# Strassen's blocks: the eight matmul units of the second FFN product stand in two groups of four in each step

## The chip, the cores and the metric

One core of one Trainium2 chip runs the kernel. The metric is the device time of one execution in microseconds, lower is better. In the profile, PE is the matmul engine (TensorE), PEld its weight loads, DVE the vector engine, ACT the scalar engine, POOL the engine that issues some DMAs, and SP the queue that issues the others.

## What is computed

The reference is a linear attention followed by a feed-forward network (FFN), in float32:

```python
# q, k, v: (8, 8, 576, 64)
q_s = exp(q - max(q, -1)); q_s /= sum(q_s, -1) + 1e-09      # per token
k_s = exp(k - max(k,  2)); k_s /= sum(k_s,  2) + 1e-09      # per column, over the sequence
kv = einsum('bhsd,bhse->bhde', k_s, v)
attn = einsum('bhsd,bhde->bhse', q_s, kv)
x = attn.transpose(0, 2, 1, 3).reshape(4608, 512)
h = x @ w_in                                  # (512, 2048)
g = h * (1.0 / (1.0 + exp(-1.702 * h)))
out = g @ w_out                               # (2048, 512)
```

## The kernel before

The 4608 tokens are worked on in nine blocks of 512 (`t` = 0 to 8). Each operand of the FFN is split into a high and a low part, and a product is three matmuls: high by high, high by low, low by high. While one block runs its FFN, the attention of the next block is computed between its matmuls.

A block's FFN has eight steps; a step handles two of the sixteen 128-wide slices of the hidden layer. In blocks 0 and 1 the first FFN product is plain (`plain1`). In blocks 2 to 8 (`t >= 2`, 56 steps) it is one level of Strassen's algorithm (`ffn1`): seven half-size products, numbered 6, 1, 2, 7, 5, 4, 3 in the order in which a step runs them, each of six matmuls of 256 columns (L889). They use only two PSUM banks, Y (bank 4) and Z (bank 5), in turn: 6 in Y, 1 in Z, 2 in Z, 7 in Y, 5 in Z, 4 in Y, 3 in Z, then the next step's 6 in Y and 1 in Z. Between two products in a bank a vector or scalar instruction reads the bank:

- after product 1, ACT copies Z to `tt` (L913), and DVE adds Y and that copy (L902, `tt<-bank,tt`);
- after product 2, ACT applies the activation to Z (L905, `g<-bank`); product 5 then starts Z anew;
- after product 7, DVE adds Y and the copy (L902, `tt<-bank,tt`); product 4 then goes on in Y;
- after products 5, 4 and 3, DVE adds the bank and a part of `tt` into `g` (L902, `g<-bank,tt`); the next products in these banks are 3, the next step's 6 and the next step's 1.

The activation (L905), the split into high part `gh` (L930, ACT) and low part `gl` (L933, DVE) follow. The second FFN product (`ffn2`) uses `gh` and `gl` one step later: eight units, one for each of four token groups `c` and two slices `jj`. A unit is three matmuls of 512 columns (L952) that add into bank `c` (0 to 3); these banks fill over the whole block and are copied out (L962) at its end.

The order of the program is made by a planner. Each piece of work is added with an engine, a cost, what it reads and writes, and a rank. The due time of a matmul piece is its place when all of them are sorted by rank. The planner then walks through time with the given costs: whenever an engine is free, the ready piece with the earliest due time goes next. Each engine executes its own list in that fixed order. The rank of a step is `R(t, step, off)`: 15 slots for each step, and `off` is a place among them. The seven products stand at slots 0, 1, 4, 6, 8, 10 and 12 (`OPS`), and the units of the step before at the values that `slots` gives:

```python
slots = iter((2, 2.3, 2.6, 6.3, 6.6, 10.3, 10.6, 13))
units = [(c, jj) for jj in range(2) for c in range(C)] if t < 2 else [(c, jj) for c in (2, 3, 0, 1) for jj in range(2)]
...
rank = R(t, step + 1, next(slots))
```

So in a step of `t >= 2` with nothing else between, the order before is 6, 1, three units, 2, 7, two units, 5, 4, two units, 3, one unit. The weights of the first product (`wj`, `wt`) lie in two sets of buffers that take turns from step to step (`wt0`, `wj00`, `wj01` and `wt1`, `wj10`, `wj11`).

Of the kernel before, what the change touches and what calls it, by code (L numbers as in the profile page):

```python
# [138 lines left out]
def efficient_attention_then_gelu_ffn(  # L139
# [168 lines left out]
    def R(t, step, off=0.0):  # L308
        return SLOTS * (NS * t + step) + off
# [7 lines left out]
    def slot(kind, p, jj):  # L317
        return f"wo{SLOT[kind][p]}{jj}"
# [38 lines left out]
    def next_tmp(n):  # L357
        nt[n] += 1
        i = nt[n] % n
        return (tmp[i] if i < 2 else wide[:, i - 2]), ("tmp", i)  # L360
# [36 lines left out]
    def pair(t, step):  # L397


        return NS - 1 - step if t % 2 else step  # L400
# [536 lines left out]
    def ffn2(t, step):  # L937
        p, gi = pair(t, step), step % 2
        ov = out[t * TB : (t + 1) * TB, :].rearrange("(p c) m -> p c m", c=C)
        slots = iter((2, 2.3, 2.6, 6.3, 6.6, 10.3, 10.6, 13))  # L940
        units = [(c, jj) for jj in range(2) for c in range(C)] if t < 2 else [(c, jj) for c in (2, 3, 0, 1) for jj in range(2)]
        opened = set()
        for c, jj in units:
            u, cs = c // 2, slice(c % 2 * P, (c % 2 + 1) * P)
            first_, last = step == 0 and c not in opened, step == NS - 1 and c in opened
            opened.add(c)

            def run(c=c, jj=jj, u=u, cs=cs, first_=first_, last=last):
                gx, gl = (gs[e][gi][:, jj, u, cs] for e in range(2))
                wh, wl = wo[p, jj][:, 0], wo[p, jj][:, 1]  # L950
                for e, (l, r) in enumerate(((gx, wh), (gx, wl), (gl, wh))):
                    nc.tensor.matmul(bank[c], l, r, start=first_ and e == 0, stop=last and e == 2)  # L952

            rank = R(t, step + 1, next(slots))
            reads = (("gs", gi, 0, u, jj), ("gs", gi, 1, u, jj), slot("wo", p, jj))
            plan.add("PE", 0.70, reads, (("bank", c),), rank, run)
            if not last:
                continue
            o, T = next_tmp(2)

            def run_o(c=c, o=o):
                (nc.vector.tensor_copy if c % 2 else nc.scalar.copy)(o, bank[c])  # L962

            def run_d(c=c, o=o):
                nc.sync.dma_start(out=ov[:, c, :], in_=o)

            plan.add("DVE" if c % 2 else "ACT", 0.65, (("bank", c),), (T,), rank - PRIOR, run_o)
            plan.add("SP", 0.4, (T,), (("out", t, c),), rank - PRIOR, run_d, size=P * DM * 4, lead=2.0)
# [49 lines left out]
    for t in range(NB):  # L1018
        if t > 1:
            at(R(t, -1, 0.5), lambda rank, t=t: x_split(t))  # L1020
        for step in range(NS):
            if t:
                at(R(t, step - 2, 0.2), lambda rank, t=t, step=step: load_kept(t, step))
            if t == 1:
                at(R(t, step, 0.1), lambda rank, step=step: sums(step))
            at(R(t, step), lambda rank, t=t, step=step: (plain1 if t < 2 else ffn1)(t, step))
            at(R(t, step + 1, 1), lambda rank, t=t, step=step: ffn2(t, step))
# [30 lines left out]
```

## Time and profile before

| | |
|---|---|
| median of 3 runs | 848.88 us (847.56 to 849.13) |
| the profiled execution | 847.62 us, of which the span on the core is 845.8 us |
| PE busy | 840.3 us, 99% of the span |
| DVE busy | 521.8 us, 62% |
| ACT busy | 482.7 us, 57% |
| granted PE clock | 0.999 of 2.4 GHz |

The profile is one execution. A matmul's row gives its start and a modelled end, so the pace of PE is read from start to start. A weight load belongs to the matmul behind it and runs while the matmul ahead of it streams.

### The profile page before, as it was taken

What the parts mean: (1) busy time and instruction counts of PE and PEld (TensorE: products, weight loads), DVE (VectorE), ACT (ScalarE), POOL (GpSimd) and SP (SyncE); (2) the same over time, 40 slices, a digit from 0 to 9 for tenths busy, and PEclk for the clock granted to TensorE, in tenths of its full rate; (3) what the DMA queues carried; (4) which work ended last, traced back from release to release, by engine and by line L of the source; (5) the groups of instructions that cost most, each with busy time, mean ns of one, the idle gap of its engine ahead of it and who ended that gap; (6) DMA issues with size and microseconds to landing.
All of it is one profiled execution on the core that took longest, in us unless ns stands there. A gap on an engine that the chain in (4) does not pass through costs nothing.

```text
span 845.8 us, 14761 instructions
## 1 busy us (share of the span) xinstructions
PE 840.3 (99%) x5685; PEld 723.8 (86%) x5685; DVE 521.8 (62%) x1077; ACT 482.7 (57%) x834; POOL 110.5 (13%) x179
## 2 busy tenths in 40 slices
PE   9999999999999999999999999999999999999997
PEld 5788778877898899889988998899988899899996
DVE  8998899989357753785368636664356533453333
ACT  6978968669239642874368634954366533353332
POOL 2001011210121001210131012101110011101110
PEclk9999999999999999999999999999999999999999
DMA  9998957891597339851895169524563165416541
GB/s 269 376 397 250 275 163 240 247 317 55 162 264 214 96 100 253 220 162 34 250 252 154 47 208 266 174 88 147 169 198 110 50 201 175 147 50 200 174 150 50
DMA packets 126278, 155.63 MB, mean 184 GB/s; under 512 B 75520, under 2 KB 104192, under 8 KB 119808
## 3 DMA queue, kind: packets, MB, share of 16 engines
q0 software_dynamic: 25248, 83.37, 32.3%
q1 hardware_dynamic: 100960, 71.32, 28.8%
q8 instruction: 45, 0.74, 0.4%
q14 instruction: 25, 0.20, 0.1%
HBM read 128.45 MB, written 26.21 MB: 183 GB/s over the span
## 4 chain that ended last, share of the span: by engine, by line
PE 99%; DMA 0%; DVE 0%; issue 0%; DVEq 0%
PE bank L952 47%; PE bank L889 33%; PE bank L842 11%; PE bank L669 3%; PE bank L748 2%; PE bank L727 2%; PE bank L304 2%; PE bank L621 1%; DMA out<-tmp 0%; DVE tmp L962 0%; DVE g L265 0%; DVE first L261 0%; DVEq L962 0%; DVE g L268 0%; DVE first L262 0%
## 5 line engine op out<-in xcount | busy, mean ns | idle before, releaser
L952 PE MATMUL bank<-w,gh 128*128 128x512 f32 x1152 | 360.1, 394 | 0.0
L952 PEld LDWEIGHTS bank<-w,gh 128*128 128x128 f32 x1152 | 199.6, 188 | 32.5 <-issue 1.9
L952 PE MATMUL bank<-w,gl 128*128 128x512 f32 x576 | 226.4, 393 | 0.0
L889 PE MATMUL bank<-xo,wt 128*128 128x256 f32 x1344 | 186.8, 281 | 0.0
L889 PEld LDWEIGHTS bank<-xo,wt 128*128 128x128 f32 x1344 | 177.1, 188 | 8.9
L905 ACT ACTIVATE g<-g 128x512 f32<-128x512 f32 x112 | 58.8, 525 | 167.1 <-DVE g L902 166.6
L889 PEld LDWEIGHTS bank<-xo,wj 128*128 128x128 f32 x1008 | 136.2, 188 | 11.1 <-ACT qt L718 1.3
L889 PE MATMUL bank<-xo,wj 128*128 128x256 f32 x1008 | 144.5, 279 | 0.0
L952 PEld LDWEIGHTS bank<-w,gl 128*128 128x128 f32 x576 | 108.3, 188 | 23.6
L902 DVE TENSOR_TENSOR g<-bank,tt 128x256 f32<-128x256 f32 x168 | 71.0, 423 | 89.5 <-PE bank L889 89.5
L410 POOL DMA_DIRECT2D wj<-kept x96 | 59.4, 619 | 468.7 <-PE bank L889 398.3
L933 DVE TENSOR_TENSOR gl<-g,gh 128x512 fp32r<-128x512 f32 x112 | 77.2, 689 | 69.7 <-ACT gh L930 69.7
L902 DVE TENSOR_TENSOR tt<-bank,tt 128x256 f32<-128x256 f32 x112 | 47.3, 422 | 115.7 <-PE bank L889 95.9
L842 PE MATMUL bank<-xp,wj 128*128 128x512 f32 x384 | 93.4, 393 | 0.0
L842 PEld LDWEIGHTS bank<-xp,wj 128*128 128x128 f32 x384 | 71.6, 188 | 18.2 <-issue 2.0
L930 ACT CAST gh<-g 128x512 fp32r<-128x512 f32 x112 | 69.6, 621 | 3.3
L905 ACT ACTIVATE g<-bank 128x256 f32<-128x256 f32 x56 | 21.6, 385 | 82.5 <-PE bank L889 82.2
L572 POOL PARTITION_ALL_REDUCE mx<-mx x32 | 27.6, 863 | 107.4 <-DVE mx L568 100.0
L410 POOL DMA_DIRECT2D wt<-kept_t x42 | 22.3, 530 | 128.1 <-PE bank L889 128.1
L913 ACT COPY tt<-bank 128x256 f32<-128x256 f32 x56 | 20.9, 373 | 24.4 <-PE bank L889 23.8
L905 ACT ACT_TABLE_LOAD x25 | 32.1, 1283 | 0.5
L718 ACT ACT_TABLE_LOAD x23 | 29.5, 1283 | 0.4
(101 smaller groups left out, 788.2 us busy)
## 6 DMA issues: line engine op xcount, KB each, us to landing
wt<-kept_t POOLq DMA_DIRECT2D x42, 1024.0 KB, 5.2
wj<-kept POOLq DMA_DIRECT2D x54, 512.0 KB, 3.6
wj<-kept POOLq DMA_DIRECT2D x42, 256.0 KB, 4.8
out<-tmp SPq DMA_DIRECT2D x36, 256.0 KB, 2.8
raw<-in_moe_w_in SPq DMA_DIRECT2D x16, 512.0 KB, 10.0
raw<-in_moe_w_out SPq DMA_DIRECT2D x16, 512.0 KB, 9.0
kept<-wj SPq DMA_DIRECT2D x16, 512.0 KB, 8.9
kept_t<-wt SPq DMA_DIRECT2D x8, 1024.0 KB, 4.9
```

The source lines that it names most:

```text
L410: "POOL", 1.0, (key,), (ring,), R(t, step - 2, off), lambda: nc.gpsimd.dma_start(out=out(), in_=src), size=size,
L572: nc.gpsimd.partition_all_reduce(flat, flat, P, bass_isa.ReduceOp.max)
L669: nc.tensor.matmul(pk[r0 : r0 + D, m, cols], lhs, rhs, start=c == 0, stop=c == len(one_) - 1, tile_position=(0, r0),)
L718: plan.add("ACT", act(e), (k,), (k,), rank, lambda y=y: nc.scalar.activation(y, y, AF.Exp), table="exp")
L842: nc.tensor.matmul(bank[bk], w[:, l, c, :], x[:, r], start=c == 0 and e == 0, stop=c == KC - 1 and e == 2)
L889: nc.tensor.matmul(ph[bk], w, x[:, r, c, :], start=opens and c == 0 and e == 0, stop=c == 1 and e == 2, skip_group_check=True,)
L902: return lambda: nc.vector.tensor_tensor(out=o, in0=ph[bk], in1=x, op=ALU.add)
L905: return lambda: nc.scalar.activation(o, x, AF.Gelu_apprx_sigmoid)
L913: vec("ACT", act(n), (ZB,), (A,), 2, lambda: nc.scalar.copy(a, ph[Z]))
L930: vec("ACT", act(2 * n), half, H, slot, lambda c=c, gh=gh: nc.scalar.copy(gh, c))
L933: nc.vector.tensor_tensor(out=gl, in0=c, in1=gh.bitcast(F32), op=ALU.subtract)
L952: nc.tensor.matmul(bank[c], l, r, start=first_ and e == 0, stop=last and e == 2)
```

## The change

One line of `ffn2`: for blocks with `t >= 2` the units get other slots, with four of them behind product 1 (slot 1) and four around slot 10 to 11, behind product 4 (slot 10). Blocks 0 and 1 keep the old slots.

```diff
     def ffn2(t, step):
         p, gi = pair(t, step), step % 2
         ov = out[t * TB : (t + 1) * TB, :].rearrange("(p c) m -> p c m", c=C)
-        slots = iter((2, 2.3, 2.6, 6.3, 6.6, 10.3, 10.6, 13))
+        slots = iter((2, 2.3, 2.6, 6.3, 6.6, 10.3, 10.6, 13) if t < 2 else (2, 2.3, 2.6, 2.9, 10.3, 10.6, 10.9, 11))
```

The planner turns this into a new order. The first place is PE in the last block, from product 2 to product 4 of a step. In the names, `bank5` is Z, `bank4` is Y, `xo10`, `xo4`, `xo5`, `xo6` are the inputs of products 2, 7, 5 and 4, and the rows of L952 are units (a unit is one row with `gh` and one with `gl`). Before:

```order
L889 MATMUL bank5_68<-xo10_1986,wj00_107 128x256 x6
L889 MATMUL bank4_67<-xo4_2053,wt0_1476 128x256 x6
L952 MATMUL bank3_66<-w_1109,gh1_78 128x512 x2
L952 MATMUL bank3_66<-w_1109,gl1_80 128x512
L952 MATMUL bank0_63<-w_1098,gh1_78 128x512 x2
L952 MATMUL bank0_63<-w_1098,gl1_80 128x512
L889 MATMUL bank5_68<-xo5_2058,wt0_1476 128x256 x6
L889 MATMUL bank4_67<-xo6_2064,wt0_1476 128x256 x6
```

The same place of the changed kernel, on PE:

```order
L952 MATMUL bank3_66<-w_1109,gh1_78 128x512 x2
L952 MATMUL bank3_66<-w_1109,gl1_80 128x512
L889 MATMUL bank5_68<-xo10_1986,wj00_107 128x256 x6
L889 MATMUL bank4_67<-xo4_2053,wt0_1476 128x256 x6
L889 MATMUL bank5_68<-xo5_2058,wt0_1476 128x256 x6
L889 MATMUL bank4_67<-xo6_2064,wt0_1476 128x256 x6
L952 MATMUL bank0_63<-w_1098,gh1_78 128x512 x2
L952 MATMUL bank0_63<-w_1098,gl1_80 128x512
```

The two units between products 7 and 5 are gone: one stands ahead of product 2 and one behind product 4, and the four products 2, 7, 5, 4 follow each other directly.

The second place is the border to the next step, on PE. `xo7` is the input of product 3; `xo8` and `xo9` are those of the next step's products 6 and 1. Before:

```order
L952 MATMUL bank1_64<-w_1098,gl1_80 128x512
L889 MATMUL bank5_68<-xo7_2079,wj01_108 128x256 x6
L952 MATMUL bank1_64<-w_1109,gh1_78 128x512 x2
L952 MATMUL bank1_64<-w_1109,gl1_80 128x512
L889 MATMUL bank4_67<-xo8_2011,wt1_1380 128x256 x6
L889 MATMUL bank5_68<-xo9_1792,wj10_109 128x256 x6
```

And of the changed kernel, on PE:

```order
L952 MATMUL bank1_64<-w_1109,gh1_78 128x512 x2
L952 MATMUL bank1_64<-w_1109,gl1_80 128x512
L889 MATMUL bank5_68<-xo7_2079,wj01_108 128x256 x6
L889 MATMUL bank4_67<-xo8_2011,wt1_1380 128x256 x6
L889 MATMUL bank5_68<-xo9_1792,wj10_109 128x256 x6
```

The unit between product 3 and the next product 6 now stands ahead of product 3, so that only product 6 lies between two products in bank Z.

The planner does not keep the pattern everywhere. The order of the changed kernel has products 2, 7, 5, 4 in direct sequence in 33 of the 56 steps. In 8 steps with attention work it has 2, 7, a unit, 4, a unit, 5; in 5 it has two units between 7 and 5; in the others a unit or attention matmuls stand between. Product 3, the next 6 and the next 1 follow directly at 25 step borders; at the others a unit, a transpose or attention matmuls stand between. SP's list is the same in both kernels, and POOL's differs in one exchange of neighbours in each of four blocks.

## Rows read from the trace of the kernel before

**Rows 1.** The page's head, the busy line, the granted PE clock in 40 slices (9 is 90% or more), and the chain of work that ended last, by engine.

```profile
span 845.8 us, 14761 instructions
PE 840.3 (99%) x5685; PEld 723.8 (86%) x5685; DVE 521.8 (62%) x1077; ACT 482.7 (57%) x834; POOL 110.5 (13%) x179
PEclk9999999999999999999999999999999999999999
PE 99%; DMA 0%; DVE 0%; issue 0%; DVEq 0%
```

**Rows 2.** The waits of PE and of its weight loads, longest first: us in total, times, longest us. "issue" is time without a wait that the profile shows.

```profile
PE bank L304 <- DVE g L268: 1.3, 1, 1.3
PEld bank L889 <- ACT qt L718: 1.3, 4, 0.5
PEld bank L889 <- issue: 0.8, 1, 0.8
```

**Rows 3.** Timeline of the last block, a step on the buffers `wt1`, `wj10`, `wj11` (start us, us, engine, line, operation, count; in brackets the idle time before and its releaser). In order: product 7, ACT's reading after product 2, the first unit, DVE's sum after product 7, products 5 and 4 in one row, the unit behind them, product 3, `gl`, the last unit, DVE's sum after product 3, the next product 6.

```profile
808.80 0.89 PE L889 MATMUL bank<-xo,wt 128*128 128x256 f32 x6
809.00 0.38 ACT L905 ACTIVATE g<-bank 128x256 f32<-128x256 f32 x1 [2.41 <-PE bank L889]
809.53 0.63 PE L952 MATMUL bank<-w,gh 128*128 128x512 f32 x2
809.73 0.42 DVE L902 TENSOR_TENSOR tt<-bank,tt 128x256 f32<-128x256 f32 x1 [2.67 <-PE bank L889]
...
810.91 1.60 PE L889 MATMUL bank<-xo,wt 128*128 128x256 f32 x12
...
812.36 0.63 PE L952 MATMUL bank<-w,gh 128*128 128x512 f32 x2
...
813.74 0.84 PE L889 MATMUL bank<-xo,wj 128*128 128x256 f32 x6
814.33 0.69 DVE L933 TENSOR_TENSOR gl<-g,gh 128x512 fp32r<-128x512 f32 x1 [1.35 <-ACT gh L930]
814.42 0.62 PE L952 MATMUL bank<-w,gh 128*128 128x512 f32 x2
...
814.94 0.42 DVE L902 TENSOR_TENSOR g<-bank,tt 128x256 f32<-128x256 f32 x1
815.11 0.84 PE L889 MATMUL bank<-xo,wt 128*128 128x256 f32 x6
```

**Rows 4.** The same view of the next step, on `wt0`, `wj00`, `wj01`: ACT's activation that follows DVE's sum of 814.94, product 1, ACT's reading after product 2, the first unit between 7 and 5, DVE's sum after product 7, products 5 and 4.

```profile
815.39 0.42 ACT L905 ACTIVATE g<-g 128x256 f32<-128x256 f32 x1 [1.09 <-DVE g L902]
815.79 0.84 PE L889 MATMUL bank<-xo,wj 128*128 128x256 f32 x6
...
819.41 0.39 ACT L905 ACTIVATE g<-bank 128x256 f32<-128x256 f32 x1 [2.37 <-PE bank L889]
819.89 0.62 PE L952 MATMUL bank<-w,gh 128*128 128x512 f32 x2
820.09 0.42 DVE L902 TENSOR_TENSOR tt<-bank,tt 128x256 f32<-128x256 f32 x1 [2.57 <-PE bank L889]
...
821.26 1.52 PE L889 MATMUL bank<-xo,wt 128*128 128x256 f32 x12
```

**Rows 5.** Timeline of the weight loads: those of the product 1 that starts at 815.79.

```profile
815.68 0.75 PEld L889 LDWEIGHTS bank<-xo,wj 128*128 128x128 f32 x6
```

**Rows 6.** Timeline of PE in a step on `wt0`, `wj00`, `wj01` that follows a stretch of attention matmuls: its product 6, its last unit (behind product 3), then the next step's products 6 and 1, where four transposes stand ahead of product 6.

```profile
417.98 0.87 PE L889 MATMUL bank<-xo,wt 128*128 128x256 f32 x6
...
427.77 0.63 PE L952 MATMUL bank<-w,gh 128*128 128x512 f32 x2
...
428.83 0.95 PE L889 MATMUL bank<-xo,wt 128*128 128x256 f32 x6
429.62 0.87 PE L889 MATMUL bank<-xo,wj 128*128 128x256 f32 x6
```

**Rows 7.** Five steps as stretches, each from the start of its product 6 to that of the next: the stretch, its length, busy time and rows of PE, PEld, DVE, ACT, POOL, then granted clock, DMA share and GB/s. The fourth uses `wt1`, `wj10`, `wj11`, the others `wt0`, `wj00`, `wj01`; the first and the last row are the first and the last of the fast steps that the prediction counts.

```profile
283.54:293.80 10.26, 10.26 (x68) 9.27 (x67) 6.38 (x15) 6.28 (x10) 0.48 (x1) 1.00 0.35 121
...
742.58:752.83 10.25, 10.25 (x68) 9.27 (x66) 6.84 (x14) 6.65 (x13) 0.00 (x0) 1.00 0.01 2
752.83:763.08 10.25, 10.25 (x67) 9.27 (x66) 4.68 (x10) 4.26 (x9) 1.31 (x3) 1.00 0.39 125
763.08:773.59 10.51, 10.51 (x68) 9.48 (x66) 4.00 (x9) 3.05 (x6) 1.79 (x4) 1.00 0.73 219
...
815.11:825.36 10.25, 10.25 (x67) 9.27 (x66) 3.31 (x8) 3.05 (x6) 0.48 (x1) 1.00 0.33 113
```

**Rows 8.** Timeline of a step with attention work, in the third block: DVE's sum after product 7, the second of two units behind product 7, then product 4 (which stands ahead of product 5 here).

```profile
266.04 0.42 DVE L902 TENSOR_TENSOR tt<-bank,tt 128x256 f32<-128x256 f32 x1 [1.17 <-PE bank L889]
...
266.52 0.62 PE L952 MATMUL bank<-w,gh 128*128 128x512 f32 x2
...
267.21 1.58 PE L889 MATMUL bank<-xo,wt 128*128 128x256 f32 x12
```

**Rows 9.** Timeline of the end of the program: the last `gl`, and the first of the last four units, which need it.

```profile
837.25 0.69 DVE L933 TENSOR_TENSOR gl<-g,gh 128x512 fp32r<-128x512 f32 x1 [1.14 <-ACT gh L930]
...
838.62 0.62 PE L952 MATMUL bank<-w,gh 128*128 128x512 f32 x2
```

## Prediction, made before the changed kernel ran

> **What bounds the kernel now.** I read the page first. PE is busy for 840.3 of 845.8 us, the clock is granted in full in every slice, and the chain that ended last is PE for 99% [rows 1]. The list of waits says the same from the other side: the only waits of PE and of the loads for the products with a named releaser come to 1.3 us each over the whole run [rows 2]. So in the 56 Strassen steps PE goes from matmul to matmul, and no other engine holds it. Two things follow. An order that does the same matmuls has no wait to remove, so it can gain little. And it can lose wherever it brings a product so close to the reader of its bank that PE has to wait. The rest is a question of how much room each product has, which the timelines of two quiet steps tell [rows 3, 4].
>
> A step takes 10.25 us on one set of weight buffers and 10.51 us on the other [rows 7]. I call them the fast and the slow pace; on the slow one a product lasts 0.72 us (810.91 to 812.36 for two), on the fast one 0.68 (815.11 to 815.79) [rows 3, 4].
>
> **What the change moves.** No instruction is added or removed. In front of product 5 two units go away, in front of the next product 6 one unit. What each product has left is the time from the end of the bank's reader to the start of the product, less the units taken out.
>
> *Product 5 waits for ACT's reading after product 2.* Slow step: ACT ends at 809.38, product 5 starts at 810.91, so there are 1.53 us; the two units take 1.38 (809.53 to 810.91); 0.15 is left [rows 3]. Fast step: 819.80 to 821.26 is 1.46, the units 1.37; 0.09 is left [rows 4].
>
> *Product 4 waits for DVE's sum after product 7.* Slow step: DVE ends at 810.15, product 4 starts one product after 810.91, at 811.63: 1.48 less 1.38 leaves 0.10 [rows 3]. Fast step: 820.51 to 821.94 is 1.43, less 1.37 leaves 0.06 [rows 4].
>
> *The next product 1 waits for DVE's sum after product 3.* DVE ends at 815.36, product 1 starts at 815.79: 0.43. Here DVE came late because `gl` held it till 815.02, while product 3 ended at 814.58; with a start 0.04 behind that end it would be 0.32 earlier. In the new order product 3 stands two units (1.38 us) further behind product 4, from which `gl` descends, so `gl` is out of the way. The unit taken out is 0.69 (814.42 to 815.11). 0.43 + 0.32 - 0.69 = 0.06 is left [rows 3, 4]. Where the product 6 between runs at the slow pace, 0.04 more: 0.10.
>
> **What a product needs.** No row shows PE waiting for ACT or DVE in such a place, so the cost is bounded from its parts. From the end of one engine's work to the start of another's that waited for it: 0.03 (815.36 to 815.39) [rows 3, 4]; with what rounding hides I take 0.04. The list of waits puts what PE waited for in the products on the weight load, not on the matmul [rows 2]. So the first load of a product is held too, and a load starts 0.11 us ahead of its matmul (815.68 to 815.79) [rows 4, 5]. That makes 0.15 us from the reader's end to the product's start. The lower bound is 0.04, if the load can go ahead of the wait. The upper bound is 0.25: behind four transposes product 6 takes 0.79 us (428.83 to 429.62) where 0.70 to 0.72 is usual, some 0.1 more for a break in the flow [rows 6].
>
> **The stalls.** With 0.15, a slow step loses 0 at product 5 and 0.05 at product 4. A fast step loses 0.06 at product 5, and at product 4 0.09 less the 0.06 already lost, 0.03. That is 0.07 a step on average; 33 steps have the four products in direct sequence: 2.3 us. Product 1 loses 0.09 or 0.05, on average 0.07; 25 borders: 1.8 us. In the 8 steps with 7, a unit, 4, the sum after product 7 ended at 266.46 and product 4 started at 267.21, 0.75 later; less one unit of 0.69 (266.52 to 267.21) leaves 0.06, so 0.09 is lost [rows 8]: 0.7 us. Three half cases (attention matmuls next to product 5) add 0.2. Sum 5.0 us.
>
> **The pace.** The second term is what a stall does behind itself. The fast buffers do not always run fast: the step at 417.98, on the fast set, follows attention matmuls that broke the flow, and from its product 6 to its last unit it takes 9.79 us (417.98 to 427.77) [rows 6]. At the fast pace that stretch is a step of 10.25 less its last unit of 0.69, 9.56 [rows 3, 7]. So a break leaves the step 0.23 us slower than the fast pace. By the starts and lengths of the products in the timeline fifteen steps, from the one at 283.54 to that at 815.11, run fast from product 6 on [rows 7]. If a stall acts like that break, they lose 0.23 each, less some 0.06 since on the slow pace the stalls are smaller: 15 x 0.17 = 2.6 us. I take it as likelier than not, as both hold the weight loads up; the bounds are 0 and 2.6.
>
> **What costs nothing.** The units wait for `gh` and `gl`; those of groups 0 and 1 move later, and those of groups 2 and 3 behind the same product 1, so none gets closer. At the end of the program product 3 moves 0.69 later, and with it the chain to the last `gl`, which loses the 0.3 us for which DVE was held; so `gl`, which ended at 837.94, would end at 838.3. The unit that needs it still starts at 838.62 and reads it in its third matmul [rows 9]. The weight DMAs that POOL issues wait for products 4 and 3; these move by one unit, 0.69, within a step of 10 us [rows 7]. Where the planner puts ACT's table loads ahead of the reading of product 2, it has kept four pieces between 2 and 5 as before.
>
> **Sum.** 5.0 + 2.6 = 7.6 us, of which 0.3 comes back since on the slow pace the first unit behind products takes 0.01 longer and there are two such borders instead of three (about 30 steps): 7.3. The profiled execution took 847.62 us, 1.8 above its span and 1.26 below the median of 848.88. On the profiled time that is 854.9, on the median 856.2; I say **856.0**.
>
> **Rivals.** *No wait at all.* If the weight load goes ahead and only the matmul waits, 0.04 is enough, less than the smallest room of 0.06. Nothing changes: 848.5 to 849.5. The rows speak against it, as they book the waits on the load [rows 2]; for it, that a load does run under the matmul ahead. The Trainium skill (TensorE: Matmul & The Clock Gate, Architectural detail) says that PE's queue can pull a weight load ahead of matmuls in flight, which favours this rival; no row here shows a load more than one matmul ahead. Chance 0.10.
>
> *A break costs more.* With 0.25 instead of 0.15, a slow step loses 0.15 at products 5 and 4 together, a fast one 0.19, product 1 0.19 or 0.15, the 8 steps 0.19: 33 x 0.17 + 25 x 0.17 + 8 x 0.19 = 11.4 us, with the pace 14: 863. For it speaks that PE has not once been seen to restart from such a wait, against it that the 0.1 was seen with a change of matmul shape. The Trainium skill (Perfetto Trace Analysis, Optimizing Tensor Performance) says that independent matmul groups should rotate through PSUM banks so that one's evacuation overlaps the next's matmuls; with two banks and one product between, that overlap is what gets short here. By that rule the change loses, but it gives no size. Chance 0.20.
>
> *Faster.* If a stall puts the slow steps on the fast pace instead, up to 28 steps gain 0.26 each, 7.3 us, against 5.0 of stalls: 846.5. It decides from 20 steps on (5.0 / 0.26). Against it speaks the broken step, which went to the slow side [rows 6]. Chance 0.04.
>
> **Numbers.** My forecast (5 to 9 us lost) has 0.66, and 856.0 is its time; its own range is 853 to 859. The range over the cases is 850 to 864, which leaves out the first and the third rival. A change of 0.2% (1.7 us) is about what a measurement of this kernel can tell from none. Slower by more: 0.66 + 0.20 = 0.86; the same: 0.10; faster: 0.04.
>
> **What would show it.** PE's list of waits would show L889 waiting for ACT g L905 and DVE tt and g L902, some 33 to 60 times each, under 0.15 us each. In a quiet step of the last block product 5 would start 0.15 us behind ACT's end and product 4 0.16 behind DVE's. The steps on the fast buffers would go from 10.25 to about 10.5 to 10.6, the slow ones from 10.51 to 10.6. If the waits are there but the steps on the fast buffers lose only the stalls, the pace term is wrong; if no waits are there, the load did go ahead. A long wait in the attention steps would mean that ACT or DVE came late there, which I cost at nothing.

## The result, and the profile after

The changed kernel takes 854.52 us (median of 6 runs, 853.75 to 854.71) where the kernel before takes 848.90 on the same chip (6 runs, 847.56 to 849.13): a ratio of 1.0070, 95% interval 1.006 to 1.008. It is slower, by 5.6 us. The profiled execution took 853.75 us.

The page of the changed kernel, its head, the busy line and the chain of work that ended last:

```profile
span 852.0 us, 14765 instructions
PE 846.4 (99%) x5685; PEld 729.1 (86%) x5685; DVE 522.9 (61%) x1077; ACT 479.1 (56%) x834; POOL 117.7 (14%) x179
PE 99%; DMA 0%; DVE 0%; issue 0%; DVEq 0%
```

Against [rows 1] the span is 6.2 us longer, and PE is "busy" for 6.1 us more with the same 5685 matmuls. So the page shows no idle engine: the loss is booked as busy time. The steps show it. Three of the last block as stretches (columns as in [rows 7]): a step on `wt0`, `wj00`, `wj01`, one on the second set, and the next on the first set.

```profile
778.55:789.12 10.57, 10.57 (x69) 9.55 (x67) 3.42 (x7) 3.01 (x6) 1.79 (x3) 1.00 0.54 174
810.29:820.88 10.59, 10.59 (x68) 9.57 (x67) 3.42 (x7) 3.02 (x6) 1.79 (x3) 1.00 0.56 169
820.88:831.44 10.56, 10.56 (x68) 9.53 (x67) 3.42 (x7) 3.01 (x6) 0.71 (x1) 1.00 0.25 83
```

Before, the first set's steps took 10.25 and the second set's 10.51 [rows 7]; they lost 0.31 and 0.08, and the two sets now run alike, at a granted clock of 1.00 as before.

Where it went, product by product. The timeline of the slow step 810.29: ACT's reading after product 2, then the first weight load of product 5; DVE's sum after product 7, then the first load of product 4 (start us, us, engine, line, operation, count; in brackets the idle time before and its releaser):

```profile
815.43 0.38 ACT L905 ACTIVATE g<-bank 128x256 f32<-128x256 f32 x1 [3.07 <-PE bank L889]
815.87 0.19 PEld L889 LDWEIGHTS bank<-xo,wt 128*128 128x128 f32 x1
816.15 0.42 DVE L902 TENSOR_TENSOR tt<-bank,tt 128x256 f32<-128x256 f32 x1 [3.07 <-PE bank L889]
816.62 0.19 PEld L889 LDWEIGHTS bank<-xo,wt 128*128 128x128 f32 x1
```

At the next border: product 6, DVE's sum after product 3, then the first loads of product 1 and its six matmuls.

```profile
820.88 0.84 PE L889 MATMUL bank<-xo,wt 128*128 128x256 f32 x6
821.08 0.42 DVE L902 TENSOR_TENSOR g<-bank,tt 128x256 f32<-128x256 f32 x1 [0.97 <-PE bank L889]
821.56 0.30 PEld L889 LDWEIGHTS bank<-xo,wj 128*128 128x128 f32 x2
821.56 0.98 PE L889 MATMUL bank<-xo,wj 128*128 128x256 f32 x6
```

And in the fast step that follows, again product 5 behind ACT and product 4 behind DVE:

```profile
826.01 0.39 ACT L905 ACTIVATE g<-bank 128x256 f32<-128x256 f32 x1 [3.07 <-PE bank L889]
826.45 0.19 PEld L889 LDWEIGHTS bank<-xo,wt 128*128 128x128 f32 x1
826.70 0.42 DVE L902 TENSOR_TENSOR tt<-bank,tt 128x256 f32<-128x256 f32 x1 [3.02 <-PE bank L889]
827.18 0.19 PEld L889 LDWEIGHTS bank<-xo,wt 128*128 128x128 f32 x1
```

Add start and length of each reader: it ends at 815.81, 816.57, 821.50, 826.40 and 827.12, and the load starts 0.06, 0.05, 0.06, 0.05 and 0.06 later. Five times out of five, on ACT and on DVE, the load is what waits. Before, the load of product 1 began at 815.68, 0.32 behind DVE's end at 815.36 [rows 3, 5], and in the same quiet steps products 5 and 4 started 1.4 us and more behind their readers [rows 3, 4]. Product 1's row shows the loss of a border in one number: its six matmuls last 0.98 where they lasted 0.84 [rows 4].

The list of waits of the weight loads hardly shows it (us in total, times, longest):

```profile
PEld bank L889 <- DVE tt L902: 2.0, 8, 0.3
```

These eight are the steps "7, a unit, 4, a unit, 5", for instance this load of product 4:

```profile
267.84 0.77 PEld L889 LDWEIGHTS bank<-xo,wt 128*128 128x128 f32 x6 [0.25 <-DVE tt L902]
```

The list counts idle time from the end of the load before, so it books 0.25 where only some 0.08 is lost (product 4 lasts 0.78 to 0.81 there, not 0.71 or 0.72); and the waits of 0.02 to 0.11 us at products 1, 5 and 4 of the other steps it doesn't list at all. A load's row lasts 0.19 and the next load starts 0.11 to 0.12 behind its start, so when a load is late by that little, the one ahead of it still counts as running or has ended at most 0.03 before.

### The profile page after: what moved, and what is told of

It reads as the page before. It is cut to its first block, busy times and chain, and to the rows that moved or that the text cites. A ratio compares the mean times of both kernels' runs of the same rounds, so it can differ in the third digit from the quotient of the medians.

```text
span 852.0 us, 14765 instructions
## 1 busy us (share of the span) xinstructions
PE 846.4 (99%) x5685; PEld 729.1 (86%) x5685; DVE 522.9 (61%) x1077; ACT 479.1 (56%) x834; POOL 117.7 (14%) x179
## 4 chain that ended last, share of the span: by engine, by line
PE 99%; DMA 0%; DVE 0%; issue 0%; DVEq 0%
PE bank L952 47%; PE bank L889 33%; PE bank L842 10%; PE bank L669 3%; PE bank L748 2%; PE bank L727 2%; PE bank L304 2%; PE bank L621 1%; DMA out<-tmp 0%; DVE tmp L962 0%; DVE g L265 0%; DVE first L261 0%; DVEq L962 0%; DVE g L268 0%; DVE first L262 0%
## 5 line engine op out<-in xcount | busy, mean ns | idle before, releaser
L952 PE MATMUL bank<-w,gh 128*128 128x512 f32 x1152 | 359.8, 393 | 0.0
L952 PEld LDWEIGHTS bank<-w,gh 128*128 128x128 f32 x1152 | 204.8, 188 | 39.2 <-issue 4.1
L952 PE MATMUL bank<-w,gl 128*128 128x512 f32 x576 | 226.2, 393 | 0.0
L889 PE MATMUL bank<-xo,wt 128*128 128x256 f32 x1344 | 186.5, 284 | 0.0
L889 PEld LDWEIGHTS bank<-xo,wt 128*128 128x128 f32 x1344 | 172.0, 188 | 4.2 <-DVE tt L902 2.0
L889 PEld LDWEIGHTS bank<-xo,wj 128*128 128x128 f32 x1008 | 137.5, 188 | 11.5 <-issue 0.8
L889 PE MATMUL bank<-xo,wj 128*128 128x256 f32 x1008 | 146.4, 280 | 0.0
L952 PEld LDWEIGHTS bank<-w,gl 128*128 128x128 f32 x576 | 108.2, 188 | 23.8
L902 DVE TENSOR_TENSOR g<-bank,tt 128x256 f32<-128x256 f32 x168 | 70.8, 423 | 78.3 <-PE bank L889 76.5
L902 DVE TENSOR_TENSOR tt<-bank,tt 128x256 f32<-128x256 f32 x112 | 47.1, 421 | 110.9 <-PE bank L889 94.8
L572 POOL PARTITION_ALL_REDUCE mx<-mx x32 | 35.4, 1105 | 106.5 <-DVE mx L568 99.4
L731 ACT COPY qT<-bank 128x512 f32<-128x512 f32 x36 | 20.7, 582 | 18.2 <-PE bank L727 17.8
```

What stands on the lines that cost most here:

```text
L572: nc.gpsimd.partition_all_reduce(flat, flat, P, bass_isa.ReduceOp.max)
L731: plan.add("ACT", act(TB), (PB,), (Q,), rank, lambda: nc.scalar.copy(qT[hp % 2], pq), lead=-2.5)
L889: nc.tensor.matmul(ph[bk], w, x[:, r, c, :], start=opens and c == 0 and e == 0, stop=c == 1 and e == 2, skip_group_check=True,)
L902: return lambda: nc.vector.tensor_tensor(out=o, in0=ph[bk], in1=x, op=ALU.add)
```

## The experiments

Seven steps of the last block, from the first set's step in which product 6 stands at 752.83 before to the one at 825.36, have no attention matmuls, so they are the yardstick: 72.53 us before, by these two starts [rows 7]. The same stretch in the changed kernel (columns as in [rows 7]):

```profile
757.50:831.44 73.94, 73.94 (x464) 66.81 (x463) 26.08 (x52) 22.66 (x45) 10.73 (x18) 1.00 0.52 164
```

In the first experiment:

```profile
756.82:830.18 73.36, 73.36 (x463) 66.37 (x462) 26.62 (x52) 22.47 (x46) 10.73 (x18) 1.00 0.53 165
```

In the second:

```profile
756.05:829.14 73.09, 73.09 (x464) 65.92 (x463) 25.90 (x52) 22.66 (x45) 10.73 (x18) 1.00 0.54 166
```

In the third:

```profile
755.00:827.54 72.54, 72.54 (x464) 65.52 (x462) 26.62 (x52) 22.50 (x46) 10.73 (x18) 1.00 0.53 167
```

**Only the places behind products 7 and 5.** Diff against the changed kernel:

```diff
-... else (2, 2.3, 2.6, 2.9, 10.3, 10.6, 10.9, 11))
+... else (2, 2.3, 2.6, 2.9, 10.3, 10.6, 10.9, 13))
```

> The last unit goes back to its old place between product 3 and the next step's product 6; the four units behind product 1, and with them product 5 and product 4 right behind products 7 and 5, stay as in the change. Theory of the bank waits: product 1 has a unit between its bank's reader and itself again, so its loss (2.6 us over the 56 steps between before and after) goes and that of products 5 and 4 (3.7 us) stays: 851.5 to 852.5 us, and a fast step of the last block goes from 10.56 to about 10.45. Rival, that the units in groups of four cost and not the waits: the groups are hardly changed, 854 to 855.

Measured: 852.66 us against 848.09 of the kernel before (ratio 1.0052, 1.0037 to 1.0067), a little above what I expected. The seven steps cost 0.83 more than before. A step on the first set and one on the second, as stretches:

```profile
756.82:767.22 10.40, 10.40 (x68) 9.40 (x67) 4.89 (x9) 4.19 (x10) 1.31 (x3) 1.00 0.46 137
767.22:777.75 10.53, 10.53 (x67) 9.53 (x66) 4.20 (x8) 3.05 (x7) 1.78 (x4) 1.00 0.75 233
```

The first set's step lost 0.15, not 0.31. The timeline of its matmuls, product 2, then products 7, 5 and 4 in one row, the unit behind them, product 3 and the unit behind it:

```profile
760.92 0.84 PE L889 MATMUL bank<-xo,wj 128*128 128x256 f32 x6
761.60 2.34 PE L889 MATMUL bank<-xo,wt 128*128 128x256 f32 x18
763.78 0.63 PE L952 MATMUL bank<-w,gh 128*128 128x512 f32 x2
...
765.85 0.84 PE L889 MATMUL bank<-xo,wj 128*128 128x256 f32 x6
766.53 0.62 PE L952 MATMUL bank<-w,gh 128*128 128x512 f32 x2
```

Product 2 takes 0.68 from start to start, and so does product 3. The three between take 2.18, 0.14 more than three times 0.68: the two stalls are 0.09 of that, and the rest is that products 5 and 4 run at the slow pace behind them. The rival of the groups put this run at 854 to 855, and the time is against it. But the group behind product 4 has one unit fewer here, so the run with another bank below, in which no unit moves, is the cleaner test.

**Only the border.**

```diff
-... else (2, 2.3, 2.6, 2.9, 10.3, 10.6, 10.9, 11))
+... else (2, 2.3, 2.6, 6.3, 6.6, 10.3, 10.6, 11))
```

> The reverse of the first: two units go back between product 7 and product 5, and the last unit stays ahead of product 3, so that only product 6 stands between product 3 and the next product 1. Theory of the bank waits: only product 1 loses, 25 to 33 times about 0.1 us: 851 to 852 us, and the two halves (this one less before, the first one less before) add up to the 5.6 us of the whole change. Rival, that one stall of a step already puts the rest of it on the slow pace: this one alone costs 4 us or more (853 and above) and the halves add up to more than the whole.

Measured: 851.57 us (1.0035, 1.0023 to 1.0048). Seven steps: 0.56 more. The two halves, 0.83 and 0.56, make 1.39 of the whole change's 1.41, so in quiet steps they add up and nothing is left for a third cause. The rival of one stall that slows the whole step falls there. The totals do not add up: 4.6 and 3.5 us make 8.1, not 5.6, which is what the rival had said. In the profiled executions the 56 steps come to 4.8 and 2.3 us more than before, against 5.6 for the whole change; another 1.5 us of this run arose ahead of them, where the program is the same (the first Strassen step starts at 215.32, in the first experiment at 213.82). So 1.5 us of the steps' sum lie outside the seven quiet ones, among them the steps whose attention work the planner orders differently in each version; where they arise was not traced.

**One unit at each place.**

```diff
-... else (2, 2.3, 2.6, 2.9, 10.3, 10.6, 10.9, 11))
+... else (2, 2.3, 2.6, 6.3, 10.3, 10.6, 10.9, 13))
```

> Three units behind product 1, one between 7 and 5, three behind 4, one behind 3: one unit of 0.69 us at each of the places that the change empties, where two stood between 7 and 5 before. Theory of the bank waits: one unit is more than the 0.16 us that a restart wants, no product waits, 848.5 to 849.5 us. Rival, that each unit taken from between 7 and 5 costs its share: half of the 3.7 us of products 5 and 4, 850.5 to 851.

Measured: 849.74 us, a ratio of 1.0017 (1.0008 to 1.0026), between the two expectations. The seven steps settle it: 72.54, not 0.02 more than before, with one unit fewer between 7 and 5. The rival falls. The rest lies outside them. In one step with attention work, which took 0.70 more than before, the planner put product 2 straight behind product 1 in the same bank. There the wait is long enough to be shown; the timeline of that run, with ACT's copy after product 1 and the load of product 2:

```profile
274.11 0.37 ACT L913 COPY tt<-bank 128x256 f32<-128x256 f32 x1 [1.34 <-PE bank L889]
...
274.53 0.77 PEld L889 LDWEIGHTS bank<-xo,wj 128*128 128x128 f32 x6 [0.67 <-ACT tt L913]
```

The load starts 0.05 behind ACT's end at 274.48, the same turnaround. What the other steps with attention work add was not traced.

**Another bank for products 5 and 3.** In the last block banks 6 and 7 are idle, so the reader of Z can be taken out of the way without moving any instruction:

```diff
+        Z5 = 6 if t == NB - 1 else Z
...
+            bk = Z5 if n in (5, 3) else bk
...
-        vec("DVE", dve(n), (ZB, TU), ((*GB, 1),), 9, plus(cb[:, 1], Z, u))
+        vec("DVE", dve(n), (ZB5, TU), ((*GB, 1),), 9, plus(cb[:, 1], Z5, u))
...
-        vec("DVE", dve(n), (ZB, TS), ((*GA, 1),), 13, plus(ca[:, 1], Z, s))
+        vec("DVE", dve(n), (ZB5, TS), ((*GA, 1),), 13, plus(ca[:, 1], Z5, s))
```

> The changed kernel, but in the last block, where bank 6 is idle, products 5 and 3 write to bank 6 in place of their own bank. So products 5 and 1 of the eight steps of that block have no reader to wait for; product 4 still waits for the sum after product 7. Order unchanged. Theory of the bank waits: product 1 goes from 0.82 to 0.71 us in a fast step (0.79 to 0.68 in a slow one), product 5 loses its 0.065, product 4 takes that on itself (0.02 to 0.09): a step of the last block takes 10.45 to 10.50 in place of 10.56 to 10.61. Rival, that the loss comes from the order itself (a flow broken by the place of the products): the steps of the last block stay at 10.56 to 10.61.

Measured (the time, 853.05 us, is of a single execution). Three steps of the last block as stretches, on the first, the second and the first set:

```profile
799.53:809.93 10.40, 10.40 (x69) 9.37 (x67) 3.42 (x7) 2.95 (x6) 1.79 (x3) 1.00 0.59 180
809.93:820.40 10.47, 10.47 (x68) 9.48 (x67) 3.42 (x7) 2.95 (x6) 1.79 (x3) 1.00 0.57 175
820.40:830.80 10.40, 10.40 (x68) 9.37 (x67) 3.42 (x7) 2.95 (x6) 0.71 (x1) 1.00 0.26 85
```

With the order of the changed kernel and only the bank changed, the steps give back 0.16 and 0.12, about half of what the order had cost on the first set and more on the second, which now takes 10.47 where it took 10.51 before the change. The timeline of the same run (its L904 and L891 are L902 and L889 of the others): the sum after product 7 and the first load of product 4, then, at the border, the sum after product 3 and the first loads of product 1:

```profile
826.07 0.42 DVE L904 TENSOR_TENSOR tt<-bank,tt 128x256 f32<-128x256 f32 x1 [2.88 <-PE bank L891]
826.55 0.19 PEld L891 LDWEIGHTS bank<-xo,wt 128*128 128x128 f32 x1
...
831.00 0.42 DVE L904 TENSOR_TENSOR g<-bank,tt 128x256 f32<-128x256 f32 x1 [0.97 <-PE bank L891]
831.40 0.31 PEld L891 LDWEIGHTS bank<-xo,wj 128*128 128x128 f32 x2
```

Product 1's load now starts at 831.40, before DVE is done at 831.42, and product 1 lasts 0.68. Product 4, whose bank has not changed, still loads 0.06 behind its reader (826.49), and the 0.15 that the first set's step still loses lie at product 4 and behind it. So the loss at products 1 and 5 is the bank's reader, shown by taking it away.

The second set's step has one thing more to show, product 1 and the first unit behind it, in the step at 804.60 before and in this run:

```profile
805.32 0.87 PE L889 MATMUL bank<-xo,wj 128*128 128x256 f32 x6
806.02 0.63 PE L952 MATMUL bank<-w,gh 128*128 128x512 f32 x2
...
810.65 0.84 PE L891 MATMUL bank<-xo,wj 128*128 128x256 f32 x6
811.33 0.62 PE L954 MATMUL bank<-w,gh 128*128 128x512 f32 x2
```

Product 1 took 0.70 before and takes 0.68 here, with no stall ahead of it.

**The pace: where `wt1` lies.** The prediction's second term was on the pace, so I looked for what makes the second set slow. One line, in the kernel before and in the changed one:

```diff
     wide = sb("wide", [P, 4, DM], tag="wt0")
+    wt(1)
```

> The kernel before with the second set's weight tile wt1 placed in SBUF right behind the first set's, in place of its old address among the tiles of x; nothing else changes. Theory that the slow pace of the second set comes from where wt1 lies: steps on that set go from 10.51 to about 10.25, 28 x 0.26 = 7 us less, 841.5 to 843. Rival, that the pace comes from the order or from what a step takes over from the one ahead: 848.5 to 849.5, and the steps alternate 10.25 and 10.51 as before.

> The changed kernel with wt1 placed as in the run beside it. If the place of wt1 makes the slow pace, this shows the stalls at the fast pace alone: about 56 x 0.2 = 6 to 11 us behind the run beside it. If it doesn't, 854 to 855.

Measured: 848.19 us (0.9999, 0.9990 to 1.0009) and 853.98 us (1.0069, 1.0052 to 1.0086), so by the times the rival holds. The steps say more. In the kernel before with `wt1` moved, a second set's step in the third block, then one of each set in the last block:

```profile
293.71:303.96 10.25, 10.25 (x67) 9.27 (x66) 7.21 (x14) 6.72 (x13) 0.00 (x0) 1.00 0.00 0
804.72:815.21 10.49, 10.49 (x67) 9.46 (x66) 3.39 (x8) 3.05 (x6) 1.79 (x4) 1.00 0.55 170
815.21:825.70 10.49, 10.49 (x67) 9.46 (x66) 3.39 (x8) 3.05 (x6) 0.46 (x1) 1.00 0.32 109
```

The second set can run fast (10.25), and the first set can run slow with nothing in its way (10.49). Both were wrong as I had put it: the address took part, but it didn't shorten the sum. In this kernel the quiet steps between two stretches of attention work all run at one pace, 10.25 around the end of the third block and 10.49 in the last, and gains and losses evened out. That they keep the pace which the attention work ahead of them left is a guess that fits.

**A unit to put the pace back.** In some steps of the changed kernel a product behind a unit came back to the fast pace. So in the kernel before I put a unit between products 6 and 1, with the old and the moved `wt1`:

```diff
-        slots = iter((2, 2.3, 2.6, 6.3, 6.6, 10.3, 10.6, 13))
+        slots = iter((2, 2.3, 2.6, 6.3, 6.6, 10.3, 10.6, 13) if t < 2 else (0.5, 2, 2.3, 6.3, 6.6, 10.3, 10.6, 13))
```

> The kernel before with one unit moved the other way: out of the group of three behind product 1 to the place between products 6 and 1, in most steps; every other place as before. No product comes nearer to the reader of its bank. Theory of the pace (in the changed kernel and in the run with two units behind 7, product 1 behind a unit goes from 0.71 to 0.68 us on the second set's buffers, and product 2 after it): 2 x 0.03 in some 20 steps on the second set, and as much in steps that came out of a break at the slow pace: 1.2 to 2.4 us less than before, 845.7 to 847 on a kernel before of 848.1. Rival, that the pace is set by the buffers alone and the place of a unit does nothing for it: 848.1, within 0.4.

> The same with wt1 behind the first set's tile. There the steps of the last block all ran at 10.49 us on both sets. If a unit between products 6 and 1 puts the pace back to fast, and no buffer makes it slow again, those steps go to 10.25, and all steps without attention work with them: 842 to 846 us. Rival, as above: 848, steps of the last block at 10.49.

Measured: 848.66 us (1.0002, 0.9993 to 1.0011) and 848.76 (1.0001, 0.9992 to 1.0009). A second set's step of the last block, with the old `wt1`:

```profile
805.24:815.76 10.52, 10.52 (x67) 9.49 (x66) 3.44 (x8) 3.05 (x6) 1.79 (x4) 1.00 0.54 174
```

And with the moved one:

```profile
805.57:816.07 10.50, 10.50 (x67) 9.46 (x66) 3.41 (x8) 3.05 (x6) 1.79 (x4) 1.00 0.55 179
```

Neither gained. The two also show that moving this unit costs nothing that can be measured where the rooms stay large.

With a unit behind each of products 6, 2, 7, 5, 4 and 3 and two behind product 1 (slots 0.5, 2, 2.3, 4.5, 6.5, 8.5, 10.5, 13), old and moved `wt1`:

> The kernel before with the units spread: one behind each of products 6, 2, 7, 5, 4 and 3 and two behind 1. Read by the quiet steps of the last block alone, since attention work falls elsewhere. If each unit lets the next product start fast, products 1, 2, 5 and 3 run at 0.68 on both sets and the second set's steps go from 10.51 to 10.35 or less; if not, 10.51.

> The same with wt1 behind the first set's tile, read by the quiet steps. If units put the pace back, all steps of the last block at 10.25; if the pace is only carried on from what came before, 10.49 or 10.25 throughout, whichever the last attention work left.

Measured, in one execution each (852.87 and 855.16 us; attention work fell elsewhere, so these are no verdict on the order): in the last block, with the old `wt1` the quiet steps took anything from 10.25 to 10.55, with the moved one all of them 10.52 or 10.53. A unit alone doesn't put the pace back; that theory has fallen.

**Another tile at the old address.** The kernel before, same instructions in the same order, tiles placed otherwise (`LATE_WJ` is 0 in the first of the two runs and 1 in the second; that tile isn't allocated with the other `wj`):

```diff
-    wj = [[sb(f"wj{i}{jj}", [P, 2, KC, P], F32R) for jj in range(2)] for i in range(2)]
+    LATE_WJ = 0
+    wj = [[None if (i, jj) == (1, LATE_WJ) else sb(f"wj{i}{jj}", [P, 2, KC, P], F32R) for jj in range(2)] for i in range(2)]
...
+    wt(1)
+    for n in range(8):
+        for jj in range(2):
+            sb("raw", [P, 2 * DM], I32, tag=f"wo{n}{jj}")
+    for n in range(8):
+        xp(n // 4, n % 4)
+    wj[1][LATE_WJ] = sb(f"wj1{LATE_WJ}", [P, 2, KC, P], F32R)
```

> The kernel before with only the places of tiles in SBUF changed, every instruction and its order as before: wt1 goes right behind the first set's tile, and wj10, which products 1 and 2 of the second set read, takes wt1's old address. Theory that weights at that address run slow, and that a product on other weights behind them comes back to the fast pace (as product 3 does before): per step on the second set only products 1 and 2 are slow, 0.07 of a us in place of 0.26, and the slow pace after a break of attention work ends in the next such step: 28 x 0.18 = 5 us, 842 to 844. Rival, that the pace is carried on and the address alone neither makes nor ends it: 848.1 to 848.5.

> The same with wj11, which product 3 of the second set reads, at wt1's old address in place of wj10. Theory of the address: only product 3 of the second set is slow, and product 6 of the next step comes back to the fast pace: 841.5 to 843.5. Rival as above: 848.1 to 848.5.

Measured: 852.96 us (1.0061, 1.0041 to 1.0081) and 853.76 us (1.0060, 1.0043 to 1.0077). The first of them, last block, second set and first set:

```profile
809.70:820.24 10.54, 10.54 (x67) 9.51 (x66) 3.40 (x8) 3.05 (x6) 1.79 (x4) 1.00 0.58 178
820.24:830.78 10.54, 10.54 (x67) 9.51 (x66) 3.40 (x8) 3.05 (x6) 0.47 (x1) 1.00 0.30 106
```

Both theories were wrong. Every quiet step of both kernels runs slow, whichever of the two tiles is placed late. By the order in which the tiles are allocated, both place `wt0` 4 KB lower, by the size of the tile taken out ahead of it, put `wt1` right behind it, and so shift the tiles of weights and of x that follow; the addresses themselves are in no trace. So the places of tiles in SBUF change the pace, by nearly as much as the whole change costs, but not through one bad address. Which tiles do it stays open. No version beat the kernel before.

## Why the prediction was right, and where its steps were not

*Order bound by PE, nothing to gain, a loss where a product meets its bank's reader:* right, and shown in two ways: in quiet steps the loss goes with a unit put back at each place, and at products 1 and 5 with the other bank.

*The turnaround of 0.15 us:* 0.05 to 0.06 from the reader's end to the load (I had 0.04), and 0.11 from there to where its matmul would follow, as I had it from [rows 4, 5]: 0.16. The rival without a wait needed the load to go ahead; in no row here does it. The Trainium skill (TensorE: Matmul & The Clock Gate, Architectural detail) has PE pull loads ahead of matmuls in flight; these rows show that a load with a wait of its own isn't pulled past that wait. The rival of 0.25 a break falls by the same rows.

*The rooms:* a fast step's loads were late by 0.11 at product 1 (821.56, where six loads at the pace of 0.68 from 820.77, the load ahead of 820.88, end at 821.45), and by 0.09 at 5 and 4 together; I had 0.09 and 0.09. A slow step lost 0.16 in all, where I had 0.10. Over the 56 steps the first matmuls of products 1, 5 and 4, from their start to that of the second, take 5.8 us more than before (2.2, 1.5 and 2.1): the stalls that I had put at 5.0.

*The pace, +2.6 less 0.3:* this is the step that failed. The mechanism is there in part: a fast step lost 0.31 with stalls of 0.20, so 0.11 came behind them, where I had 0.17. But only eight of the fifteen fast steps lost 0.31 to 0.34. Six lost 0.03 to 0.16: in them units still stand at one of the two places, the border or between products 7 and 5, so that one of the stalls is missing (one more step, into which the planner moved an attention piece, can't be compared). Nor does the slow pace always last to the end of the step, as I had it: in the first experiment stalls of 0.09 at 5 and 4 cost the step 0.15, and product 3 runs at 0.68 again. And the other direction, which I had only as a rival with a chance of 0.04, is there too: the slow step at 810.29 lost 0.08 with stalls of 0.16. Its product 2 before, where the step starts at 804.60, and in the changed kernel, with the row of the products behind it:

```profile
808.10 0.87 PE L889 MATMUL bank<-xo,wj 128*128 128x256 f32 x6
...
814.55 0.84 PE L889 MATMUL bank<-xo,wj 128*128 128x256 f32 x6
815.23 2.38 PE L889 MATMUL bank<-xo,wt 128*128 128x256 f32 x18
```

It took 0.70 before (to 808.80 [rows 3]) and takes 0.68 after. That the stall does this is not shown; with the other bank product 1 runs fast on the second set without one. Over the 56 steps everything but those first matmuls, with what the planner moved around the attention work, comes to -0.1 us, not +2.3: 5.7 in all where the sum said 7.3. So I came out 1.5 us high on the median, with stalls 0.8 too small and a pace term 2.4 too large; that the two errors have opposite signs is luck. The other 0.5 of the span's 6.2 us arose ahead of the first Strassen step, where the program is the same.

*What would show it:* the step lengths came as said (10.25 to 10.56, 10.51 to 10.59). The list of waits did not: it has no row for ACT's reading and eight for DVE's. By my own rule that would have meant that loads went ahead, which was the wrong test; the start of the load beside the reader's end is the right one.

*Costed at nothing:* the weight DMAs, the end of the program and the units' own waits cost nothing that the steps show. The rule of the Trainium skill (Perfetto Trace Analysis, Optimizing Tensor Performance), to rotate independent matmul groups through PSUM banks, spoke against the change; the run with bank 6 now puts a number on it here, 0.12 to 0.16 us a step.

## What to carry to other kernels

With two banks in turn, a product here needed its bank's reader to end 0.16 us before it would start; count that room in units of other work before moving any, for one unit of 0.69 at each place hid it in the quiet steps. When a saturated engine gets slower by its own busy time, compare the lengths of equal rows (0.98 for 0.84) and the load's start with the reader's end, not the list of waits. And before charging a change with a slower pace, look whether the pace goes both ways. Set aside, too, what arises ahead of the changed part: with the same program there, the first Strassen step began 1.5 us later in the second experiment's profiled execution than in the first's.

## What was not expected of the hardware

The same 128x256 matmuls run at a full granted clock of 1.00 at one of two paces, 0.68 us a product or 0.70 to 0.72, and can keep it for nine steps on end, as the last ones of the kernel before with `wt1` moved do. Moving tiles in SBUF by some KB, with no instruction changed, moved whole steps from 10.25 to 10.54 and the kernel from 848.68 to 852.96 us. Neither a unit between products nor `wt1` taken off the suspected address ended it; its cause was not found.
